# A pooled-attention and routed-experts kernel: record writes taken at a denser rhythm, and a first stage in another order

## The chip, the core and the metric

The kernel runs on one core of a Trainium2 chip. The metric is the device time of one execution in microseconds (us); the time before is the median of three runs. The profile is of one further execution. In it PE is TensorE (PEld its weight loads), DVE VectorE, ACT ScalarE, POOL GpSimd, SP SyncE; L637 is line 637 of the kernel.

## The reference

Eight batches of eight heads, 576 tokens, head dimension 64. Keys and values are averaged over blocks of eight tokens, so each query attends to 72 pooled keys:

```
k_p, v_p = means of k and v over 8 tokens          # 72 x 64 per head
attn     = softmax(q @ k_p.T / 8)
x        = attn @ v_p, heads side by side           # 4608 tokens x 512
noisy    = x @ w_gate + log(1 + exp(x @ w_noise)) * noise      # 8 experts
top2, w  = the two largest of noisy, softmax of the two
out[t]   = sum over the token's two experts of w * relu(x[t] @ w1[e]) @ w2[e]
```

Inputs and output are float32; w1 is 512 x 1024 and w2 1024 x 512 for each expert.

## The kernel before

The kernel has two large stages that overlap at their seam.

**Attention and routing.** The batches are taken in four pairs (pair 0 to 3), each pair in nine chunks (ci 0 to 8) of 128 tokens, 36 chunks in all. For a chunk, `qtr` turns q on TensorE and ScalarE copies it out (`qT`); `qk` makes scores for three groups of heads, VectorE takes the maximum (`mx`, L380) and ScalarE the exponentials; `et` turns these; `av` (L408) multiplies by values and, in the same matmul, by values already multiplied with the gate and noise weights, so that VectorE writes both the rows of x (`xr`, L419) and the router's partial logits (`lg`, L421). The rows go to DRAM (`x_dram`). The gate and noise weights reach that matmul through `wr` (loaded by `mid_consts`, L190) and `wrb`, six GpSimd copies of it (L196).

When a pair's last chunk is reached, `route` starts as a generator that is advanced two steps per chunk. GpSimd adds the heads' logits (L508, L509: "the adds"); VectorE begins at L516 and goes on through top-2; at L593 TensorE counts, for each token, its place in its expert's list (`rk`); VectorE then makes the records (L634 is its last instruction). For each pair there are 18 **record writes** (L637): indirect DMAs that GpSimd issues one by one, each of 128 records. They are put into a list, `scq`, from which `advance(n, m)` takes at most m at a time. Behind the writes of pairs 1, 2 and 3 stand, in the same list, the **record load** (L678) and the **row gathers** (L705) of expert 0's groups 0, 1 and 2: these groups take tokens only from the pairs already routed. A record write waits for a VectorE or ScalarE instruction of its chunk (`pace`).

**Experts.** For each expert there are three groups of up to four tiles of 128 rows. `split` (through `rows_of`) turns the gathered rows on TensorE (L755) and makes a high and a low part; `stage1` is x @ w1 in eight steps f (12 matmuls each, L1016); `stage2` is h @ w2, one tile t at a time (24 matmuls, L1127; L1093 for the last group of an expert). Expert 0's group 0 is turned in chunks 34 and 35 of the attention stage; groups 1 and 2 are turned from `hook`, inside stage 2 of the group before. The hooks `hook1` (per f) and `hook` (per t) also take records from `scq`, `hook1` as many as `POPS` says.

**Order.** The framework lays down each engine's instruction order when the program is built: by the order of the text, by readiness as it estimates it, and by explicit edges: `tc.issue_after(ins)` puts what is written under it behind `ins` on the same engine. On the chip every engine runs its list in order. So an instruction that waits holds up all behind it on its engine. GpSimd's list mixes adds, record writes, record loads and gathers; all loads of the first stage go through the SP queue in the order of the text.

With the pops as written, before the change, the list runs so: the 18 writes of pair 1 are taken from pair 2's ci 4 to pair 3's ci 4, ten of them before pair 2's adds are written into GpSimd's list; group 0's record load and gathers come at pair 3's ci 4; 11 writes of pair 2 come before the end of attention, the other 7, then group 1's load and gathers, in f 0 to 2 of group 0's stage 1; pair 3's 18 writes come in stage 2 of group 0 (5, 4, 4, 4) and at the head of group 1's stage 1 (1), there followed by group 2's load and gathers.

Of the kernel before, what the change touches and what calls it, by code (L numbers as in the profile page):

```python
# [8 lines left out]
F32 = mybir.dt.float32  # L9
# [4 lines left out]
OP = mybir.AluOpType  # L14
AX = mybir.AxisListType.X
# [4 lines left out]
def kernel(  # L20
# [12 lines left out]
    nc = tc.nc  # L33
# [149 lines left out]

    wrb = cp.tile([P, NSLOT, 2 * E], F32, name="wrb")

    def mid_consts():
        wr = cp.tile([P, H, 2 * E], F32, name="wr")
        for dup in range(2):
            for i, w in enumerate((moe_w_gate, moe_w_noise)):
                nc.sync.dma_start(wr[dup * 64:dup * 64 + 64, :, i * E:(i + 1) * E],  # L190
                                  w.rearrange("(h d) e -> d h e", d=D))
        nc.gpsimd.memset(wrb, 0.0)
        for n in range(NEB):
            rs = slice((n % 2) * 64, (n % 2) * 64 + 64)
            ns = len(HEADS[n])
            nc.gpsimd.tensor_copy(wrb[rs, SLOT0[n]:SLOT0[n] + ns, :],  # L196
                                  wr[rs, HEADS[n][0]:HEADS[n][0] + ns, :])

    KT, VT, QT, QR = {}, {}, {}, {}
    lastl, lasta = [None], [None]  # L200

    DK, DV = 0, 0
    PK, PV = 0, 0
# [75 lines left out]
    def v_prep(b):  # L279
        vt = VT[b]  # L280
        vs = ap_.tile([P, NEB, D], F32, tag="vs", name=f"vs{b}")
        VS[b] = vs
        if PV >> b & 1:
            halves(vt, b, BST, ((0, 3), (3, 6)), PV)
            yield
        yield from pooled(vs[:BST], vt, b, 0, NEB, BST, DV | PV)

    def pe_prep(b):
        ks = KS[b]
# [44 lines left out]
    def qtr(u, half, hp=None):  # L334
        kind, pr, b, jp = u
        if half == 0:
            QTT[u] = ap_.tile([P, H, P], F32, tag="qT", name=f"qT{pr}_{b}_{jp}", bufs=2)
        elif kind == "R":
            return
        qT = QTT[u]  # L340
        qp = ps2.tile([P, 4, P], F32, tag="one", name=f"qp{pr}_{b}_{jp}_{half}", bufs=2)
        for i in range(4):
            if kind == "R":
                src = QR[pr][:, 2 * i:2 * i + 2]
            else:
                src = QT[b][:, half * 4 + i, 2 * jp:2 * jp + 2]
            nc.tensor.transpose(qp[:, i], src.rearrange("p a d -> p (a d)"), ident)  # L347
        with tc.high_priority(offset=HP if hp is None else hp):
            nc.scalar.copy(qT[:, half * 4:half * 4 + 4], qp)

    def qk(u, g):
# [5 lines left out]
        if kind == "R":  # L357
            if g == 2:
                return
            if g == 0:  # L360
                SR[u] = [ps2.tile([P, 512], F32, tag="s", name=f"s{nm}_{k}", bufs=SB) for k in range(2)]
                for i in range(4):
                    for b2 in range(2):
                        for k in range(2):
                            nc.tensor.matmul(SR[u][k][b2 * 64:b2 * 64 + 64, i * G:(i + 1) * G],
                                             qT[k * 64:k * 64 + 64, i, b2 * 64:b2 * 64 + 64],
                                             kbd[b2][k * 64:k * 64 + 64, 2 * i + k, k * G:(k + 1) * G],
                                             start=True, stop=True)
            s = SR[u][g]
            rows = [(0, 2 * i + g) for i in range(4)]  # L370
        else:
            s = ps2.tile([P, 512], F32, tag="s", name=f"s{nm}", bufs=SB)
            rows = [(jj, h) for h in GRP[g] for jj in range(2)]
            for i, h in enumerate(GRP[g]):
                nc.tensor.matmul(s[:, i * 2 * G:(i + 1) * 2 * G], qT[:, h], kbd[b % 2][:, h],  # L375
                                 start=True, stop=True)
        n = len(rows)
        sv = s[:, :n * G].rearrange("p (r g) -> p r g", g=G)
        mx = ap_.tile([P, 6], F32, tag="mx", name=f"mx{nm}", bufs=4)
        nc.vector.tensor_reduce(out=mx[:, :n], in_=sv, axis=AX, op=OP.max, negate=True)  # L380
        for i, (jj, h) in enumerate(rows):
            lasta[0] = nc.scalar.activation(ex[:, jj, EPOS[h] * G:(EPOS[h] + 1) * G], sv[:, i], AF.Exp,  # L382
                                            bias=mx[:, i:i + 1])
# [103 lines left out]
    def drain(g):  # L487
        for _ in g:
            pass
# [322 lines left out]
    if WU:  # L812
        wu = ps2.tile([P, 512], F32, tag="s", name="wu", bufs=SB)
        for i in range(WU):
            nc.tensor.transpose(wu[:, i % 4 * P:(i % 4 + 1) * P], ident, ident)
    load_q(0)
    load_qr(0)
    load_v(0)
    block_tiles()
    mid_consts()  # L820
    drain(k_prep(0))
    load_k(1)
    load_q(1)
# [32 lines left out]
    for x in range(4):  # L856
        plan(34 + x // 2, lambda: next(splits))
    qtr(units[0], 0)
    qtr(units[0], 1)
    for g in range(3):  # L860
        qk(units[0], g)
    if ST & 1:
        qtr(units[1], 0, H0)
        qtr(units[1], 1, H0)
    drain(v_prep(0))
    if ST & 2:
        next(pg[0])
    else:
# [6 lines left out]
    for i, (ui, u, jj) in enumerate(chunks):  # L875
# [15 lines left out]

        def adv():
            pace[0] = lastx[0]
            advance(STEPS[pr], 2 if pr == NP - 1 and ci > 3 else quiet)

        for o in order + ("" if "b" in order else "b") + ("" if "x" in order else "x"):
            if o == "v" and i == 0:
# [58 lines left out]
    def split(grp):  # L956
        drain(rows_of(grp, bank))
# [192 lines left out]
                    wgens.pop(0)  # L1150

    s0 = SP_[0]
    POPS = {0: (4, 4, 2, 0, 0, 0, 0, 0), 1: (100, 0, 0, 0, 0, 0, 0, 0)}

    def hook1(i, f):
        if i == 0 and f == 0:
# [5 lines left out]
        advance(0, POPS[i][f])  # L1162

    def hook(i, t, mm):
        advance(0, (5, 4, 4, 4)[t] if i == 0 else 100)
        if t == 1 - i:
            with tc.issue_after(mm.ins):
                split(groups[i + 1])

    def flush(f):  # L1170
        if f == 3:
# [142 lines left out]
```

## Time and profile before

| | |
|---|---|
| median of three runs | 1024.56 us (1023.23 to 1025.97) |
| the profiled execution | 1026.55 us |
| its span, first to last instruction | 1024.7 us |
| granted clock of TensorE, mean | 0.990 |
| attention stage, first scores to the first matmul of L1016 | about 14 to 190.5 us |
| expert stage | 190.5 us to the end |

A row of a timeline gives the start in the span, the duration, the engine, the line, the operation, output<-inputs, and in brackets the idle time of the engine just before it with what ended it. Rows that follow one another on one engine and line are merged (x8 is eight instructions). A window row gives each engine's busy time in a stretch; the granted clock is a share of the full 2.4 GHz, so that 0.50 is the lower level of 1.2 GHz.

### The profile page before, as it was taken

The page shows a single profiled execution, that of the slowest core. Times are in us where ns is not written, and L with a number is a line of the kernel's source. Part 1 is how long each engine was busy: PE and PEld are TensorE (multiplying, and loading weights), DVE is VectorE, ACT ScalarE, POOL GpSimd, SP SyncE. Part 2 cuts the span into 40 slices and gives each one's busy share as a digit, 9 for nine tenths or more (in the row PEclk, how much of TensorE's full clock was granted, in tenths as well). Part 3 has the DMA queues.
Part 4 walks back from the last instruction along what each step waited for, and adds up shares of the span by engine and source line. Part 5 has one row for each costly group of instructions (what it writes and reads, how often), then busy time and mean ns, then how long its engine had stood idle before and what let it go on. Part 6 is the DMA issues. An engine that isn't in the chain of part 4 may idle for free.

```text
span 1024.7 us, 16468 instructions
## 1 busy us (share of the span) xinstructions
PE 990.3 (97%) x5832; PEld 886.4 (86%) x5832; DVE 548.3 (54%) x1261; ACT 344.1 (34%) x857; POOL 379.4 (37%) x433
## 2 busy tenths in 40 slices
PE   6999999898999999999999999999999999999996
PEld 5898898788898989898988898989888988898995
DVE  5799898572244455644464446444644455356341
ACT  4687787331113222411142124211421232123120
POOL 3023575646300442155115421551154215422514
PEclk9999999899899999999999999999999999999999
DMA  8989983361706755677267736772677357744624
GB/s 240 251 236 270 251 265 117 111 196 39 216 28 205 211 178 155 197 235 210 75 193 224 225 117 200 249 215 73 184 241 245 94 173 250 239 145 135 211 87 136
DMA packets 136006, 187.61 MB, mean 183 GB/s; under 512 B 29123, under 2 KB 84052, under 8 KB 135898
## 3 DMA queue, kind: packets, MB, share of 16 engines
q1 hardware_dynamic: 110458, 119.09, 39.9%
q0 software_dynamic: 25440, 67.05, 21.1%
q8 instruction: 72, 1.18, 0.5%
q14 instruction: 36, 0.29, 0.1%
HBM read 123.31 MB, written 70.74 MB: 189 GB/s over the span
## 4 chain that ended last, share of the span: by engine, by line
PE 82%; DMA 5%; DVE 4%; issue 3%; SPq 2%; POOL 2%; ACT 1%; POOLq 0%; DVEq 0%; ACTq 0%
PE bank L1016 34%; PE bank L1127 25%; PE bank L1093 10%; PE a L408 5%; PE s L375 3%; PE ep L393 2%; DMA wst<-in_moe_w_dram 2%; PE qp L347 1%; DMA xg<-x_dram,raw 1%; DMA qr<-in_q_dram 1%; DVE w L481 1%; SPq L219 1%; SPq L190 1%; POOL out_dram L1072 1%; DMA slot_dram<-ys 1%
## 5 line engine op out<-in xcount | busy, mean ns | idle before, releaser
L1016 PE MATMUL bank<-xh,w 128*128 128x512 f32 (+6 forms) x1536 | 390.4, 338 | 1.3 <-DVE pv L1064 1.3
L1016 PEld LDWEIGHTS bank<-xh,w 128*128 128x128 f32 x1536 | 270.3, 188 | 22.0 <-DVE pv L1064 1.7
L1127 PE MATMUL bank<-w,hh 128*128 128x512 f32 x880 | 272.7, 391 | 0.0
L1016 PE MATMUL bank<-xl,w 128*128 128x512 f32 (+6 forms) x768 | 259.7, 338 | 0.0
L1027 ACT ACTIVATE hh<-bank 128x512 fp32r<-128x512 f32 (+4 forms) x192 | 97.1, 508 | 458.4 <-PE bank L1016 435.0
L1028 DVE SCALAR_TENSOR_TENSOR hl<-bank,hh 128x512 fp32r<-128x512 f32 (+4 forms) x192 | 110.9, 579 | 242.8 <-ACT hh L1027 242.8
L1127 PEld LDWEIGHTS bank<-w,hh 128*128 128x128 f32 x880 | 165.9, 189 | 34.0
L1127 PE MATMUL bank<-w,hl 128*128 128x512 f32 x440 | 172.1, 391 | 0.1
L1016 PEld LDWEIGHTS bank<-xl,w 128*128 128x128 f32 x768 | 144.6, 188 | 10.3
L1064 DVE SCALAR_TENSOR_TENSOR pv<-bank,raw,pv 128x128 f32<-128x128 f32 x196 | 55.5, 342 | 109.6 <-PE bank L1127 61.9
L1068 POOL DMA_DIRECT2D slot_dram<-yt x17 | 9.8, 575 | 268.9 <-DVE yt L1064 217.4
L1093 PE MATMUL bank<-hh,w 128*128 128x240 f32 (+3 forms) x512 | 103.4, 298 | 2.1 <-DVE hl L1028 1.3
L1127 PEld LDWEIGHTS bank<-w,hl 128*128 128x128 f32 x440 | 83.0, 189 | 17.8 <-DVE hl L1028 0.5
L637 POOL DMA_INDIRECT rec_dram<-rec,pos x72 | 77.2, 1072 | 48.9 <-issue 14.2
L1048 POOL DMA_INDIRECT pv<-slot_dram,raw x70 | 68.5, 979 | 66.8 <-DMA slot_dram<-ys 34.9
L481 DVE TENSOR_TENSOR w<-wst,w 128x512 fp32r<-128x512 f32 x128 | 82.6, 682 | 10.4 <-ACT w L480 10.2
L1093 PEld LDWEIGHTS bank<-hh,w 128*128 128x128 f32 x512 | 82.5, 189 | 2.7 <-ACT hh L1027 1.6
L480 ACT CAST w<-wst 128x512 fp32r<-128x512 f32 x128 | 72.8, 618 | 27.5 <-DMA wst<-in_moe_w_dram 27.5
L714 POOL DMA_INDIRECT row<-x_dram,raw x70 | 70.0, 1000 | 21.9 <-issue 19.5
L1068 POOL DMA_DIRECT2D slot_dram<-pv x55 | 31.7, 577 | 123.7 <-DVE pv L1064 95.8
L1093 PE MATMUL bank<-hl,w 128*128 128x320 f32 (+3 forms) x256 | 75.9, 296 | 0.0
L382 ACT ACTIVATE ex<-s,mx 128x72 f32<-128x72 f32 x288 | 70.7, 344 | 9.7 <-DVE mx L380 9.6
(162 smaller groups left out, 1031.4 us busy)
## 6 DMA issues: line engine op xcount, KB each, us to landing
wst<-in_moe_w_dram SPq DMA_DIRECT2D x64, 512.0 KB
via<-row SPq DMA_DIRECT2D x266, 64.0 KB
xg<-via SPq DMA_DIRECT2D x63, 256.0 KB
slot_dram<-pv POOLq DMA_DIRECT2D x55, 256.0 KB, 3.7
x_dram<-xr SPq DMA_DIRECT2D x16, 512.0 KB
q<-in_q_dram SPq DMA_DIRECT2D x7, 1024.0 KB
k<-in_k_dram SPq DMA_DIRECT2D x6, 896.0 KB
v<-in_v_dram SPq DMA_DIRECT2D x12, 432.0 KB
```

What stands on the lines that cost most here:

```text
L382: lasta[0] = nc.scalar.activation(ex[:, jj, EPOS[h] * G:(EPOS[h] + 1) * G], sv[:, i], AF.Exp, bias=mx[:, i:i + 1])
L480: nc.scalar.copy(hv, sv)
L481: nc.vector.tensor_sub(lv, sv, hv.bitcast(F32))
L637: s = nc.gpsimd.indirect_dma_start(out=rec_dram[:, :], out_offset=bass.IndirectOffsetOnAxis(ap=pos[:, i, c:c + 1], axis=0), in_=rec[:, c, ...
L714: turn_of("pool", lambda: nc.gpsimd.indirect_dma_start(out=row[:32 * nr], out_offset=None, in_=x_dram[:, :], in_offset=bass.IndirectOffset ...
L1016: nc.tensor.matmul(part(ph), w1s(e, a, db, f), part(xs[b][:, db]), start=(i == 0), stop=(i == 3 * NDB - 1))
L1027: act = nc.scalar.activation(hh[:, :n], ph[:, :n], AF.Relu)
L1028: last = nc.vector.scalar_tensor_tensor(hl[:, :n], ph[:, :n], 0.0, hh[:, :n].bitcast(F32), op0=OP.max, op1=OP.subtract)
L1048: turn_of("pool", lambda: nc.gpsimd.indirect_dma_start(out=pv[:np_], out_offset=None, in_=slot_dram[:P + e * CAP, :], in_offset=bass.Indir ...
L1064: nc.vector.scalar_tensor_tensor(r_, y_, wc, pv[:plain] if plain else r_, op0=OP.mult, op1=OP.add)
L1093: nc.tensor.matmul(part(py), w2s(e, b, f)[:, mb * P:(mb + 1) * P], part(hs[f][a]), start=(i == 0), stop=(i == 3 * NFB - 1))
L1127: mm = nc.tensor.matmul(py, hs[f][a][:, cs], w2s(e, b, f), start=(i == 0), stop=(i == 3 * NFB - 1))
```

## The change

Three things are changed.

1. **First stage.** The gate and noise weights are no longer loaded in turned form (`wr`, four DMAs of 64 partitions x 8 heads x 8 values). They are loaded in rows of 512 values on eight partitions, twice side by side (four DMAs, right behind batch 0's v, into two of the buffers `wst`), and turned by 16 small TensorE transposes into one PSUM bank, from which one ScalarE copy makes `wr`; the six copies to `wrb` stay. The load of v of batch 0 is issued ahead of that of `qr`. The scores of the first three heads of the first unit are put in front of the transposes of q's second half; v of batch 0 is pooled in three parts (nine VectorE instructions in place of three), behind the maximum of the second head group.
2. **Rhythm of the record writes.** From pair 2 on, `adv` takes two records per chunk where it took one (in pair 3 already from ci 1). `POPS` for group 0's stage 1 becomes (8, 0, 0, 2, 3, 3, 3, 3).
3. **`hook`.** `split` of the next group is written ahead of `advance`, and after t = 0 of group 0 everything left in the list is taken.

With the pops as written, after the change: the 18 writes of pair 1 run from pair 2's ci 3 to pair 3's ci 1, 16 of them ahead of pair 2's adds; group 0's load and gathers come at pair 3's ci 1 and ci 2; 16 writes of pair 2 come before the end of attention, 2 more and group 1's load and gathers at f 0; pair 3's writes come at f 3 to f 7 (14) and t 0 (4), group 2's record load at t 0, its gathers at t 1 of group 0.

```diff
-    def mid_consts():
+    def mid_loads():
+        wt = [wp.tile([P, 2 * D * E], F32, tag="wst", name=f"wt{i}", bufs=WS) for i in range(2)]
+        for t, w in zip(wt, (moe_w_gate, moe_w_noise)):
+            for u in range(2):
+                nc.sync.dma_start(t[:H, u * D * E:(u + 1) * D * E], w.rearrange("(h d) e -> h (d e)", d=D))
+        nc.gpsimd.memset(wrb, 0.0)
+        return wt
+
+    def mid_consts(wt):
         wr = cp.tile([P, H, 2 * E], F32, name="wr")
-        for dup in range(2):
-            for i, w in enumerate((moe_w_gate, moe_w_noise)):
-                nc.sync.dma_start(wr[dup * 64:dup * 64 + 64, :, i * E:(i + 1) * E],
-                                  w.rearrange("(h d) e -> d h e", d=D))
-        nc.gpsimd.memset(wrb, 0.0)
+        wp_ = ps2.tile([P, 512], F32, tag="one", name="wps", bufs=2)
+        wv = wp_[:, :2 * E * H].rearrange("p (c h) -> p c h", h=H)
+        for i in range(2):
+            src = wt[i][:H].rearrange("h (d e) -> h e d", e=E)
+            for e in range(E):
+                nc.tensor.transpose(wv[:, i * E + e], src[:, e], ident[:H, :H])
+        nc.scalar.copy(wr, wv.rearrange("p c h -> p h c"))
...
-        yield from pooled(vs[:BST], vt, b, 0, NEB, BST, DV | PV)
+        for n0, n1 in ((0, 2), (2, 4), (4, 6)) if b == 0 else ((0, NEB),):
+            yield from pooled(vs[:BST, n0:n1], vt, b, n0, n1, BST, DV | PV)
...
     load_q(0)
+    load_v(0)
+    wt = mid_loads()
     load_qr(0)
-    load_v(0)
     block_tiles()
-    mid_consts()
...
     qtr(units[0], 0)
-    qtr(units[0], 1)
-    for g in range(3):
-        qk(units[0], g)
-    if ST & 1:
-        qtr(units[1], 0, H0)
-        qtr(units[1], 1, H0)
-    drain(v_prep(0))
+    qk(units[0], 0)
+    with tc.issue_after(lastqk[0].ins):
+        qtr(units[0], 1)
+    qk(units[0], 1)
+    mx1 = lastmx[0]
+    qk(units[0], 2)
+    qtr(units[1], 0, H0)
+    qtr(units[1], 1, H0)
+    with tc.issue_after(lastqk[0].ins):
+        mid_consts(wt)
+    with tc.issue_after(mx1.ins):
+        drain(v_prep(0))
...
-            advance(STEPS[pr], 2 if pr == NP - 1 and ci > 3 else quiet)
+            advance(STEPS[pr], 2 * quiet if pr >= NP // 2 else quiet)
...
-    POPS = {0: (4, 4, 2, 0, 0, 0, 0, 0), 1: (100, 0, 0, 0, 0, 0, 0, 0)}
+    POPS = {0: (8, 0, 0, 2, 3, 3, 3, 3), 1: (100, 0, 0, 0, 0, 0, 0, 0)}
...
     def hook(i, t, mm):
-        advance(0, (5, 4, 4, 4)[t] if i == 0 else 100)
         if t == 1 - i:
             with tc.issue_after(mm.ins):
                 split(groups[i + 1])
+        advance(0, (5, 100, 100, 100)[t] if i == 0 else 100)
```

## Rows read from the trace of the kernel before

**Rows 1.** The page's part on engines: busy time, share of the span, instructions.

```profile
PE 990.3 (97%) x5832; PEld 886.4 (86%) x5832; DVE 548.3 (54%) x1261; ACT 344.1 (34%) x857; POOL 379.4 (37%) x433
```

**Rows 2.** TensorE's timeline, 160 to 400: start, us, group, [idle before <- releaser].

```profile
177.09 0.43 PE L393 MATMUL ep<-ident,ex 128*112 128x128 f32 x2
...
181.91 1.95 PE L755 MATMUL xp<-ident,xg 128*128 128x128 f32 x8 [4.38 <-DMA xg<-x_dram,raw]
...
187.95 1.23 PE L755 MATMUL xp<-ident,xg 128*128 128x128 f32 x8
...
201.73 0.20 PE L593 MATMUL bank<-mb,before 128*128 128x80 bf16 x1
```

**Rows 3.** Timeline of all engines, 248 to 264.

```profile
252.97 0.39 PE L1127 MATMUL bank<-w,hl 128*128 128x512 f32 x1
...
261.46 1.13 PE L755 MATMUL bank<-ident,xg 128*128 128x128 f32 x4 [0.76 <-DMA xg<-x_dram,raw]
...
262.24 1.20 PE L1127 MATMUL bank<-w,hh 128*128 128x512 f32 x2
```

**Rows 4.** Windows: each engine's busy time, then granted clock, DMA share, GB/s.

```profile
184.00:185.00 1.00, 1.00 (x5) 1.00 (x4) 0.84 (x2) 1.00 (x3) 0.69 (x2) 0.50 0.43 151
...
264.00:265.00 1.00, 1.00 (x4) 0.71 (x3) 0.00 (x0) 0.00 (x0) 0.17 (x1) 0.50 0.78 221
```

**Rows 5.** GpSimd's timeline, 100 to 420.

```profile
131.13 0.97 POOL L637 DMA_INDIRECT rec_dram<-rec,pos  x1 [6.54 <-ACT eT L395]
132.41 2.45 POOL L637 DMA_INDIRECT rec_dram<-rec,pos  x1 [0.30 <-issue]
...
145.74 0.97 POOL L637 DMA_INDIRECT rec_dram<-rec,pos  x1 [0.30 <-issue]
...
146.73 3.50 POOL L508 TENSOR_TENSOR lg<-lg 128x512 f32<-128x512 f32 x2
...
168.60 0.97 POOL L637 DMA_INDIRECT rec_dram<-rec,pos  x1 [3.65 <-ACT ex L382]
...
171.05 0.59 POOL L678 DMA_DIRECT2D raw<-rec_dram  x1 [1.48 <-DMA rec_dram<-rec,pos]
...
174.52 1.00 POOL L705 DMA_INDIRECT xg<-x_dram,raw  x1 [0.30 <-issue]
...
190.48 1.30 POOL L508 TENSOR_TENSOR lg<-lg 128x512 f32<-128x512 f32 x1
...
213.37 0.58 POOL L678 DMA_DIRECT2D raw<-rec_dram  x1 [4.43 <-DMA rec_dram<-rec,pos]
...
217.99 1.00 POOL L705 DMA_INDIRECT xg<-x_dram,raw  x1 [4.04 <-DMA raw<-rec_dram]
...
247.90 0.96 POOL L637 DMA_INDIRECT rec_dram<-rec,pos  x1 [0.31 <-issue]
...
253.14 1.00 POOL L705 DMA_INDIRECT xg<-x_dram,raw  x1 [4.28 <-PE bank L1127]
...
256.99 0.95 POOL L705 DMA_INDIRECT xg<-x_dram,raw  x1 [0.31 <-issue]
```

**Rows 6.** VectorE's timeline, 118 to 250: three steps of routing.

```profile
153.02 0.23 DVE L516 SCALAR_TENSOR_TENSOR rt<-rt 128x72 f32<-128x72 f32 x1 [0.62 <-POOL rt L509]
...
170.87 0.15 DVE L634 TENSOR_TENSOR rec<-rt,tok 128x18 int32<-128x18 f32 x1
...
195.17 0.23 DVE L516 SCALAR_TENSOR_TENSOR rt<-rt 128x72 f32<-128x72 f32 x1 [3.12 <-POOL rt L509]
```

**Rows 7.** Windows of four microseconds in the first stage, columns as in rows 4.

```profile
16.00:20.00 4.00, 2.63 (x17) 2.25 (x16) 2.41 (x3) 3.19 (x13) 0.96 (x1) 1.00 0.71 74
...
20.00:24.00 4.00, 2.73 (x20) 2.23 (x19) 3.63 (x8) 2.63 (x10) 2.20 (x6) 1.00 1.03 386
```

**Rows 8.** Timeline of all engines, 0 to 45.

```profile
13.16 1.09 PE L347 MATMUL qp<-ident,q 128*128 128x128 f32 x4 [1.36 <-DMA q<-in_q_dram]
...
15.73 0.61 DVE L380 TENSOR_REDUCE mx<-s 128x6 f32<-128x432 f32 x1 [4.67 <-PE s L375]
...
19.04 3.22 POOL L196 COPY wrb<-wr 64x32 f32<-64x32 f32 x6 [12.17 <-DMA wr<-in_moe_w_noise_dram]
...
28.13 0.63 PE L347 MATMUL qp<-ident,qr 128*128 128x128 f32 x4 [0.34 <-DMA qr<-in_q_dram]
```

More of the change, by code (lines that the diff above doesn't have):

```diff
@@ L199 @@
     KT, VT, QT, QR = {}, {}, {}, {}
-    lastl, lasta = [None], [None]
+    lastl, lasta, lastqk, lastmx = [None], [None], [None], [None]
     DK, DV = 0, 0
@@ L346, in qtr @@
                 src = QT[b][:, half * 4 + i, 2 * jp:2 * jp + 2]
-            nc.tensor.transpose(qp[:, i], src.rearrange("p a d -> p (a d)"), ident)
+            lastqk[0] = nc.tensor.transpose(qp[:, i], src.rearrange("p a d -> p (a d)"), ident)
         with tc.high_priority(offset=HP if hp is None else hp):
@@ L374, in qk @@
             for i, h in enumerate(GRP[g]):
-                nc.tensor.matmul(s[:, i * 2 * G:(i + 1) * 2 * G], qT[:, h], kbd[b % 2][:, h],
-                                 start=True, stop=True)
+                lastqk[0] = nc.tensor.matmul(s[:, i * 2 * G:(i + 1) * 2 * G], qT[:, h], kbd[b % 2][:, h],
+                                             start=True, stop=True)
         n = len(rows)
@@ L379, in qk @@
         mx = ap_.tile([P, 6], F32, tag="mx", name=f"mx{nm}", bufs=4)
-        nc.vector.tensor_reduce(out=mx[:, :n], in_=sv, axis=AX, op=OP.max, negate=True)
+        lastmx[0] = nc.vector.tensor_reduce(out=mx[:, :n], in_=sv, axis=AX, op=OP.max, negate=True)
         for i, (jj, h) in enumerate(rows):
```

## The prediction

> **What bounds the kernel now.** I read the page first, then TensorE's timeline, then the lists of the engines that it waits for. The page says that TensorE is busy for 97% of the span [rows 1]; so what can be won lies in the rest, and in work done at the low clock. In the timeline of the seam and of expert 0, TensorE waits long in two places.
>
> *Stall 1, group 0's rows.* TensorE ends a group at 177.52 and then waits 4.38 us, to 181.91, for the gather of x rows [rows 2]. After it the granted clock is 0.50 [rows 4]; with that level up to about 187.5 the 5.6 us from 181.91 on do the work of half, so 2.8 us more are lost. Price: 7.2 us.
>
> *Stall 2, group 2's rows.* Stage 2 of group 1 ends its first tile at 253.36; the next begins at 262.24 [rows 3]. In these 8.9 us lie 16 transposes; eight take 1.23 us at the full clock [rows 2], so 16 take 2.5 and 6.4 us are waiting. Behind it the clock is again at 0.50 [rows 4], up to about 266, which loses half of 3.8 us, 1.9. Price: 8.3 us.
>
> Both wait for GpSimd's list. Group 0's record load is at 171.05, its first gather at 174.52; group 2's last record write ends at 248.86, the gathers go from 253.14 to 256.99, and the last lands at 261.45, 4.5 us after its issue [rows 3, 5]. The stages after that keep TensorE full, so what is won at 262 should arrive at the end.
>
> The third place is the start: VectorE idles 4.67 us before the first maximum at 15.73 [rows 8], and the DMA engines move 74 GB/s in 16 to 20 although they are 71% busy, against 386 GB/s in the next four microseconds [rows 7]; there the weights' 2048 pieces of 32 bytes are under way.
>
> **The change part by part.**
>
> *First stage.* Removed: the loads in small pieces. What stands behind them in SP's queue (k, q and the rest of q of batch 1) can land earlier, but the wait that shows is small, 0.34 us at 28.13 [rows 8]. Scores first: the transposes of q's second half wait for q until 13.16, and the first maximum follows 2.6 us later; with scores that need only q's first half, up to these 2.6 us come off VectorE's idle time. Added: 16 transposes (0.15 us each at most [rows 2], 2.5 together, where TensorE has 1.4 us idle of 4 [rows 7]), one ScalarE copy, and six more VectorE instructions; the smallest step of routing takes 0.23 us [rows 6], so 1.4 at most. The six copies to `wrb` remain, 3.22 us from 19.04 on [rows 8]; their cause is now TensorE's transposes behind the second unit's, and not a load, so they hardly begin earlier. Ends: 3.9 us lost, if nothing hides the new work, to 4.7 won, if the whole idle time goes. I take 2.0 won, nearest to the 2.6 of the scores.
>
> *Stall 1.* Group 0's load and gathers move up by two to three chunks. GpSimd then does, from 131.13 on, 16 writes of pair 1, pair 2's adds, two writes, the load, four gathers. Ten writes took 15.6 us here (131.13 to 146.73), 1.56 each; a write in a quiet stretch takes 0.96 + 0.31 = 1.27 [rows 5]. So: 25.0 + 6.3 (adds, 146.73 to L516 at 153.02 [rows 5, 6]) + 2.5 + load 0.9 and its two waits, 1.5 before it and 2.6 behind it (3.5 from issue to gather, less the 0.9) = 38.8: the first gather goes at 169.9 and not at 174.5, and with its 7.3 us of flight (174.52 to about 181.8 [rows 2, 5]) lands at 177.2, just ahead of TensorE's 177.5. Stall 1 goes: 7.2.
>
> *Stall 2.* Pair 3's writes move up from stage 2 into stage 1 of group 0, but GpSimd's list is one queue, and becomes dense. I sum it from 131.13 to group 2's gathers: 16 writes at 1.56 (25.0), 38 at 1.27 (48.3), adds of pair 2 6.3, of pair 3 3.4 (190.48 to 195.17, less a write inside), ten gathers at 1.28 (12.8), two loads and, priced like them, the stores of two tiles' rows that stand in between, at 0.9 each (3.6), and the waits around the loads: 4.1, 4.43 + 4.04, and 4.28 for group 2 [rows 5, 6], 16.9 in all. That is 116.3 us; the last gather goes at 246.2 and lands at 250.6, against 261.45: 10.9 earlier. TensorE without stall 1 would be there at 253.36 - 7.2 = 246.2; it still waits some 2.6 us in pieces, and ends the transposes at 251.3, 10.9 before 262.24. Whether the clock falls in that remnant decides over another 0 to 1.9; I take 0.
>
> *What is late next.* Six more writes stand ahead of pair 2's adds in GpSimd's list. VectorE's first routing step (L516, 153.02) waited 0.62 us for them [rows 6], so it is at its limit now. Behind it on VectorE stand maxima and rows of x, for which ScalarE and TensorE wait. Call the extra wait D. If the order that the build lays down foresees none of it, D is 6 x 1.56 = 9.4; if it foresees all, 0. I take what an order reckoned at the quiet price would miss, 6 x (1.56 - 1.27) = 1.7. D moves attention, and the rest of GpSimd's list with it, one for one.
>
> Sum: 10.9 + 2.0 - 1.7 = 11.2 us. The profiled execution took 1026.55 us, 1.85 more than its span and 2.0 more than the median; so 1015.4 on its terms, and **1013.4 us** on the median's. In general the time is 1011.7 + D.
>
> *A rule against the change.* While pair 1's records are written and VectorE is at its fullest, the spacing of the writes is 1.56 us on the mean, and one took 2.45; in the quiet stretch it is 1.27 [rows 5]. The Trainium skill, SBUF — State Buffer, section "Who interferes with whom", says that GpSimd and VectorE share a port pair under an exclusive lock, and that a DMA issued from GpSimd stalls for want of descriptors while VectorE holds it. By that rule the denser writes of pairs 1 and 2 should each wait for VectorE; the trace agrees in direction, with 0.29 us each, and at that the rule changes nothing in the sum above. It has its case below.
>
> **The rivals.**
>
> *Both stalls gone whole.* For it: if the 16 writes keep the quiet spacing, the list is 16 x 0.29 = 4.6 us shorter, and TensorE at 246.2 finds the rows there. Against it: TensorE's count (`rk`, 201.73 [rows 2]) comes right behind VectorE's chain that begins at 195.17 after waiting 3.12 us for GpSimd [rows 6]; without stall 1 TensorE is there 7 us earlier. Won: 7.2 + 8.3 + 2.0 = 17.5; 1007.1.
>
> *Given back on VectorE.* D near 9.4, because L516 keeps its place in VectorE's list: 1021.1. Or the same size at `rk`, where pair 3's adds stand behind 14 writes of pair 2 that can't begin before their records exist, at 171.0 [rows 6]: 171.0 + 14 x 1.27 = 188.8, about as late as before, so that the 7.2 of stall 1 come back at 201.7. For it: the order of writes ahead of adds is seen in the trace (145.74, then 146.73 [rows 5]).
>
> *Slower: the writes stretch.* Place: GpSimd's 16 writes ahead of pair 2's adds. If each took what the longest took, 2.45 + 0.30 [rows 5], they would need 44 us in place of 15.6, D would be 28 and the time 1040. It decides from D = 12.9, a spacing of 1.78 us (16 x 1.78 - 15.6), for slower than before, and from 1.97 us for slower by 0.3%. For it: ten writes already vary between 0.97 and 2.45. Against it: the mean. The Trainium skill's rule on the shared port (SBUF — State Buffer, "Who interferes with whom") would have this outcome if VectorE held the port through most of each write.
>
> *No change.* The gathers don't come earlier, since a record write waits for an instruction of its chunk anyway (3.65 us for an exponential at 168.60 [rows 5]), and the start gains nothing: 1024.6.
>
> **How the numbers follow.** A difference of 0.3% (3.1 us: 1021.5 and 1027.6) is about what a measurement of this kernel can tell from none. Chances: forecast, D from 0 to 5, 1010 to 1017: 0.45. Both stalls gone whole, 1004 to 1010: 0.20. Given back, 1017 to 1023: 0.20, a third of it above 1021.5. No change: 0.08. Slower: 0.07. So faster 0.45 + 0.20 + 0.13 = 0.78, same 0.07 + 0.08 = 0.15, slower 0.07. The range must leave out 0.2: above it, no change, slower and the end of given back, 0.15 to 0.18; below it, the best of both stalls gone with the start's full 4.7: 1007.1 - 2.7 = 1004.4. I give 1004.5 to 1022.0; the forecast's own range is 1010 to 1017.
>
> **What the profile after would show.** Right: TensorE's wait before the first transposes of group 0's rows under 1 us and no granted clock of 0.50 there; group 0's gather some 5 us earlier; the second wait down from 6.4 us to about 3, its gathers at 240 to 247; the first maximum at about 13.4. Wrong: L516 of pair 2 waiting over 5 us for GpSimd's adds, with TensorE idle behind it; `rk` of pair 3 with several us of idle in front; write spacings of 1.8 us and more in pairs 1 and 2; the first `av` later than now, which would put the fault in the weights' new way through TensorE, ScalarE and GpSimd.

## The result, and the profile after

The changed kernel takes 1030.18 us (median of 11 runs, 1026.85 to 1036.64) where the kernel before takes 1024.56 in the same set (11 runs): ratio 1.0064, 95% interval 1.0043 to 1.0084. It is slower by some 6 us; the forecast was 1013.4.

The profiled execution took 1030.17 us. The head of its page (first part of each line: busy us, share of the span, instructions), against [rows 1]:

```profile
span 1028.2 us, 16508 instructions
...
PE 992.4 (97%) x5848; PEld 891.4 (87%) x5848; DVE 546.4 (53%) x1267; ACT 343.5 (33%) x858; POOL 374.7 (36%) x433
```

TensorE is busy 2.1 us longer, part of it at the low clock, and the span is 3.5 us longer. Where the waits are now, in TensorE's timeline of the changed kernel, is to be read against [rows 2, 3]:

```profile
158.13 1.22 PE L376 MATMUL s<-kbd,qT 64*64 64x72 f32 x14 [5.90 <-ACT ex L393]
...
184.90 1.23 PE L766 MATMUL xp<-ident,xg 128*128 128x128 f32 x8 [0.26 <-ACT eT L406]
...
209.21 0.23 PE L604 MATMUL bank<-mb,before 128*128 128x80 bf16 x1 [6.88 <-DVE mb L577]
```

Both stalls of before are gone: the transposes of group 0's rows wait 0.26 us for an eviction and no longer for the gather, and between 211 and 287 no idle time over 0.5 us is left. In their place stand two new waits, 5.90 us at pair 2's scores and 6.88 us at the count of pair 3. Who is waited for is one step back, in VectorE's timeline (L527 is the routing step that was L516 in [rows 6]):

```profile
156.97 0.23 DVE L527 SCALAR_TENSOR_TENSOR rt<-rt 128x72 f32<-128x72 f32 x1 [6.46 <-POOL rt L520]
...
202.65 0.23 DVE L527 SCALAR_TENSOR_TENSOR rt<-rt 128x72 f32<-128x72 f32 x1 [9.96 <-POOL rt L520]
```

The same two steps waited 0.62 and 3.12 us before. L520 is the last of the routing adds on GpSimd; what stands ahead of them is GpSimd's timeline, against [rows 5]:

```profile
129.52 0.98 POOL L648 DMA_INDIRECT rec_dram<-rec,pos  x1 [7.25 <-DVE rec L645]
...
152.45 0.97 POOL L648 DMA_INDIRECT rec_dram<-rec,pos  x1 [0.30 <-issue]
153.45 2.06 POOL L519 TENSOR_TENSOR lg<-lg 128x512 f32<-128x512 f32 x2
155.59 0.45 POOL L520 TENSOR_TENSOR rt<-lg 128x128 f32<-128x128 f32 x1
...
162.05 0.59 POOL L689 DMA_DIRECT2D raw<-rec_dram  x1 [1.44 <-DMA rec_dram<-rec,pos]
164.96 1.02 POOL L716 DMA_INDIRECT xg<-x_dram,raw  x1 [2.32 <-DMA raw<-rec_dram]
...
178.42 1.01 POOL L648 DMA_INDIRECT rec_dram<-rec,pos  x1 [6.49 <-DVE rec L645]
...
197.96 1.30 POOL L519 TENSOR_TENSOR lg<-lg 128x512 f32<-128x512 f32 x1
...
252.83 0.95 POOL L716 DMA_INDIRECT xg<-x_dram,raw  x1 [0.30 <-issue]
```

Sixteen writes stand from 129.52 to 153.4, so pair 2's adds begin at 153.45 and not at 146.73; the late routing delays pair 2's records to 178.42 (before: 171.95), and pair 3's adds, behind fifteen writes of them, begin at 197.96 and not at 190.48. The gathers gain what was meant: group 0's first at 164.96 (before 174.52), group 2's last at 252.83 (before 256.99).

The waits cost more than their own length. Windows of the changed kernel (the number behind the five engines is the granted clock):

```profile
150.00:160.00 10.00, 4.10 (x42) 3.27 (x41) 2.62 (x9) 3.86 (x16) 7.34 (x11) 0.75 0.18 63
160.00:170.00 10.00, 10.00 (x64) 9.17 (x63) 6.41 (x30) 5.58 (x17) 5.09 (x6) 0.74 0.36 114
200.00:210.00 10.00, 3.12 (x22) 2.42 (x21) 5.95 (x27) 3.42 (x10) 5.75 (x11) 0.81 0.01 0
210.00:220.00 10.00, 10.00 (x39) 8.07 (x39) 10.00 (x38) 6.46 (x13) 2.81 (x3) 0.85 0.59 192
```

With the clock at 1.2 in place of 2.4 GHz for a time behind each wait, 160 to 170 lost 2.6 us (0.26 of ten) and 210 to 220 lost 1.5; the busy ends of the windows ahead of them (158.13 to 160 and 209.21 to 210, taken at half) lost 0.9 and 0.4, so 5.4 in all.

A third place is new: ahead of expert 1's last second stage TensorE stops for 3.48 us, and VectorE, which is named, had done its work (its last `hl` at 392.38).

```profile
391.06 0.27 PE L1032 MATMUL bank<-xh,w 128*128 128x240 f32 x1
394.81 0.75 PE L1109 MATMUL bank<-hh,w 128*128 128x240 f32 x2 [3.48 <-DVE xt L772]
```

The kernel before has a short stop near there, 0.74 us, 2.6 us into that second stage:

```profile
395.55 0.49 PE L1093 MATMUL bank<-hh,w 128*128 128x240 f32 x2 [0.74 <-issue]
```

The clock falls here too, in the changed kernel and not in the one before:

```profile
392.00:394.00 2.00, 0.00 (x0) 0.00 (x0) 2.00 (x3) 0.60 (x1) 0.00 (x0) 0.99 0.99 260
394.00:396.00 2.00, 1.19 (x5) 1.22 (x6) 1.89 (x4) 0.64 (x2) 0.00 (x0) 0.50 0.62 196
398.00:400.00 2.00, 2.00 (x11) 2.00 (x11) 1.01 (x2) 0.40 (x1) 0.00 (x0) 0.50 0.01 4
```

It is 0.50 from 394 to 400, which costs some 2.6 us more (half of the 5.2 from 394.81 on).

So far one can see that both stalls were won, and that two waits and a pause came for them. The seam comes out even: the first copy `hh` of expert 0's third group, ScalarE's first output of a group's first stage, comes at 271.6 us in the changed kernel and 271.8 in the one before. At expert 1's third group the changed kernel is 1.8 us ahead (382.0 and 383.8), and at expert 2's first 3.5 behind (411.5 and 408.0), as at the end. So in these two executions the two waits used up what the stalls gave, and the third place makes the whole of the loss. Which part of the change brings what is the experiments' to say.

### The profile page after: what moved, and what is told of

It reads as the page before. It is cut to its first block, busy times and chain, and to the rows that moved or that the text cites. A ratio compares the mean times of both kernels' runs of the same rounds, so it can differ in the third digit from the quotient of the medians.

```text
span 1028.2 us, 16508 instructions
## 1 busy us (share of the span) xinstructions
PE 992.4 (97%) x5848; PEld 891.4 (87%) x5848; DVE 546.4 (53%) x1267; ACT 343.5 (33%) x858; POOL 374.7 (36%) x433
## 3 DMA queue, kind: packets, MB, share of 16 engines
q8 instruction: 72, 1.18, 0.5%
## 4 chain that ended last, share of the span: by engine, by line
PE 87%; POOL 4%; issue 3%; DMA 3%; DVE 2%; ACT 1%; SPq 0%; POOLq 0%; ACTq 0%; DVEq 0%
PE bank L1032 37%; PE bank L1143 28%; PE bank L1109 10%; PE a L419 4%; PE s L386 2%; PE ep L404 2%; POOL rec_dram L648 2%; PE qp L358 1%; DMA wt<-in_moe_w_gate_dram 1%; DMA rec_dram<-rec,pos 1%; POOL lg L519 1%; POOL out_dram L1088 1%; PE s L376 1%; DMA k<-in_k_dram 0%; PE kT L309 0%
## 5 line engine op out<-in xcount | busy, mean ns | idle before, releaser
L1109 PE MATMUL bank<-hh,w 128*128 128x240 f32 (+3 forms) x512 | 105.9, 303 | 4.8 <-DVE xt L772 3.5
L1109 PEld LDWEIGHTS bank<-hh,w 128*128 128x128 f32 x512 | 84.9, 194 | 5.3 <-ACT xh L777 3.6
```

The lines of the kernel that those rows point to most:

```text
L1109: nc.tensor.matmul(part(py), w2s(e, b, f)[:, mb * P:(mb + 1) * P], part(hs[f][a]), start=(i == 0), stop=(i == 3 * NFB - 1))
```

## The experiments

Four sets of kernels, each with the kernel before in it. In the first two sets every kernel that the others repeat took 1.1 to 1.6% longer than there. Their traces show pauses of single engines, at different moments between some 95 and 270 us, that nothing in the trace explains (in `before_again` TensorE 1.30 us at 102.0, VectorE 1.51 at 140.6 and ScalarE 2.23 at 265.9; in `rhythm_only` TensorE 3.36 at 200.4). So each is compared with before of its own set, and points in time with those of its set alone. Two landmarks serve throughout: the first copy `hh` of ScalarE in expert 0's groups 0, 1 and 2 (they show how the seam is left), and the stretch E1 from the first `hh` of expert 1's third, last group to that of expert 2's first, in which the third place lies (the expectation of `before_dummy16` names it by the second and the third group; its numbers are those of this stretch).

**Set 1: the parts alone.** The theory: dense writes ahead of the adds make the loss. The rival: the first stage does.

`start_only`: the changed kernel's first stage, with

```diff
-            advance(STEPS[pr], 2 * quiet if pr >= NP // 2 else quiet)
+            advance(STEPS[pr], 2 if pr == NP - 1 and ci > 3 else quiet)
-    POPS = {0: (8, 0, 0, 2, 3, 3, 3, 3), ...
+    POPS = {0: (4, 4, 2, 0, 0, 0, 0, 0), ...
```

and `hook` as before. 

> The kernel before with the new first stage alone (weights turned on TensorE, scores first, v of batch 0 in parts); the order of the record writes is that of before. Theory (the loss comes from the record writes that stand ahead of the routing adds in GpSimd's list): no idle time of 5 us at the scores near 158 and none at the count rk near 205; 1 us or so won at 119, so 1022 to 1025, within 0.3% of before. Rival (the first stage costs, through TensorE, ScalarE or the late weights): 1028 or more, with the loss visible before 119.

`rhythm_only`: before, with these three places as in the change. 

> The kernel before with the new rhythm of the record writes alone (two for each step in pairs 2 and 3, other numbers in expert 0, group 2's gathers ahead of a step's writes); the first stage is that of before. Theory: TensorE waits about 6 us at pair 2's scores near 158 (the adds of pair 2 stand behind 16 writes) and about 7 us at rk near 209; the waits of before at 182 and 257 to 262 are gone; about the time of the changed kernel plus the 1 us of the start, 1028 to 1033. Rival (the first stage costs): 1021 to 1026.

`adv_alone`: the changed kernel with `POPS` and `hook` of before. 

> The changed kernel with the numbers and the order in expert 0 (POPS and hook) put back; the two writes for each step in pairs 2 and 3 stay. Theory: the waits near 158 (about 6 us) and at rk (about 7 us) stay, because the writes ahead of the adds are the same; the wait for group 2's rows (before: 6.4 us) comes back in part or whole, as pair 3's writes go out later; 1030 to 1037, slower than the changed kernel or equal. Rival (the loss comes from the numbers in expert 0, whose writes crowd the stages there): the wait at rk shrinks and the time falls to 1022 to 1026.

`hooks_alone`: the changed kernel with the `advance` line of before. 

> The changed kernel with the number of writes for each step in pairs 2 and 3 put back to that of before; first stage and the numbers in expert 0 stay. Theory: no wait of 6 us near 158, the wait for group 0's rows near 182 is back at about 4 us, rk without a wait above 2 us, and group 2's rows earlier by some us; 1016 to 1023, faster than before. Rival (the numbers in expert 0 cost): a wait of 5 us or more in expert 0 that neither kernel before has, 1027 or more.

Measured, ratio to before (1039.82 us) with its interval, then the landmarks in us:

| kernel | ratio | groups 0, 1, 2 | E1 |
|---|---|---|---|
| start_only | 1.0053 (1.0033 to 1.0074) | 208.7, 256.6, 285.6 | 25.6 |
| rhythm_only | 1.0094 (1.0068 to 1.0119) | 222.1, 272.0, 297.0 | 24.3 |
| adv_alone | 1.0139 (1.0106 to 1.0172) | 218.4, 264.7, 294.0 | 27.3 |
| hooks_alone | 1.0036 (1.0012 to 1.0060) | 206.4, 258.6, 285.3 | 25.7 |

Both held in part. The two kernels with two writes for each step enter expert 0 some 10 to 16 us later than the two without. But the way is not the one that I expected: in both, VectorE's first routing step of pair 2 waits 0.42 us for the adds, and the count of pair 3 doesn't wait at all. TensorE stands 7.50 us ahead of the second rows of group 0, and has pauses of 1 to 3 us without a releaser. So this set shows that the denser writes come with a late seam, and not by which wait. `hooks_alone` was to be faster than before by the theory (1016 to 1023), and is 0.4% slower; but `start_only`, which has the same first stage, is slower by no less without the numbers of expert 0, so these cost nothing that can be seen. The first stage alone is slower by some 5 us, which I had put at 1 us won: the rival is right too.

**Set 2: the same chip for before, after and the first stage; and a first cure.**

`before_again`, `after_again` and `start_again` repeat three kernels. 

> The kernel before, unchanged, for a profile taken on the same chip as the other kernels of this set. All theories: the two waits of before (for group 0's rows, 4 to 5 us, and for group 2's rows, about 6 us in all) stand in it.

 

> The changed kernel, unchanged, beside the kernel before on the same chip. Theory (the record writes ahead of the routing adds): ratio to before 1.004 to 1.009 again, with the waits near 158 (about 6 us) and at rk (about 7 us); the 3.5 us ahead of expert 1's last group at 395 are chance and need not come again. Rival (that wait in expert 1 belongs to the change): it comes again at the same place with 3 us or more.

 

> The kernel before with the new first stage alone, once more, now with a profile of before from the same chip. If the first stage itself costs: TensorE behind before by 3 us or more already at the first unit's end (before 60 us), ratio 1.005 again. If it gains its 1 us and the loss comes later, by the moved order of instructions: level with before or ahead of it at 60 us, and 4 us or more behind at 200. If the loss was of that chip alone: a ratio within 0.3% of 1.

`pair1_single_rk_late`: two edits of the changed kernel,

```diff
-            advance(STEPS[pr], 2 * quiet if pr >= NP // 2 else quiet)
+            advance(STEPS[pr], 2 * quiet if pr == NP - 1 else quiet)
 ...
         elif i == 0:
             next(rt, None)
-            next(rt, None)
```

> The changed kernel with two edits: pair 1's records are again written one for each step (ten ahead of pair 2's adds in place of sixteen), and the count rk of pair 3 stands two eighths of group 0's first stage later on TensorE. Theory: no wait of 5 us near 158, rk's wait under 3 us, group 0's rows with a wait under 2 us, group 2's rows without one; some 12 us less than the changed kernel, 0.6 to 1.0% faster than before. Rival (the denser writes as such cost, or the first stage does): a time within 3 us of the changed kernel.

| kernel | ratio to before (1036.28 us) | groups 0, 1, 2 | E1 |
|---|---|---|---|
| before_again | (one run, 1038.44 us) | 207.2, 251.5, 282.6 | 25.1 |
| after_again | 1.0043 (1.0018 to 1.0068) | 216.1, 258.5, 282.7 | 27.2 |
| start_again | 1.0037 (1.0015 to 1.0058) | 208.3, 255.2, 283.8 | 27.3 |
| pair1_single_rk_late | 1.0051 (1.0028 to 1.0074) | 215.0, 263.2, 288.0 | 27.7 |

`before_again` is a single run, read for its trace alone. The changed kernel enters expert 0 8.9 us late and has it all back at group 2 (in the first profiles 204.0 against 196.5, then 271.6 against 271.8); here too the loss comes in expert 1: 0.4 us ahead at its third group, 1.7 behind at expert 2's first. The two waits of 6 and 7 us that I expected to find again aren't there: VectorE's first routing steps wait 0.42 us in pair 2 and 2.95 in pair 3, and TensorE stands 4.98 us ahead of the second rows of group 0. The instructions and their order are those of the first profile, so the same program loses its time in these sets at other places, and what sets off the pauses may hide the waits. The 3.48 us in expert 1 did not come back in that size, but E1 is again longer than before's. My cure, from which I expected 0.6 to 1.0% less than before, failed: group 0 is 1.1 us earlier than in `after_again`, and groups 1 and 2 are 5 us later. That fits the list, in which eight writes now stand behind the adds and ahead of group 0's record load:

```profile
176.89 0.59 POOL L689 DMA_DIRECT2D raw<-rec_dram  x1 [2.49 <-DMA rec_dram<-rec,pos]
177.47 0.13 POOL L576 MEMSET mb<- 128x8 bf16 x1
180.00 1.01 POOL L716 DMA_INDIRECT xg<-x_dram,raw  x1 [2.40 <-DVE rec L597]
...
186.95 1.00 POOL L648 DMA_INDIRECT rec_dram<-rec,pos  x1 [2.16 <-ACT eT L406]
```

Its first gather goes at 180.00 where `after_again` has it at 175.4. In this run the adds and the gathers traded places. Part of this loss may be the set's pauses (VectorE stops 1.41 and 0.84 us, without a releaser, in pair 2's routing); since the wait at pair 2's scores that the cure was to take away is not in `after_again` either, the run, within 1 us of it as the rival had it, decides nothing.

**Set 3: the adds out of the list, and the first stage's instructions.**

`after_adds_vec`: the changed kernel, `before_adds_vec`: the kernel before, both with

```diff
-                nc.gpsimd.tensor_add(lg[:, a:b, :h], lg[:, a:b, :h], lg[:, a:b, h:2 * h])
+                V.tensor_add(lg[:, a:b, :h], lg[:, a:b, :h], lg[:, a:b, h:2 * h])
-            nc.gpsimd.tensor_add(L[:, a - c0:b - c0], lg[:, a:b, 0], lg[:, a:b, 1])
+            V.tensor_add(L[:, a - c0:b - c0], lg[:, a:b, 0], lg[:, a:b, 1])
```

> The changed kernel with the routing adds on VectorE in place of GpSimd, so that no record write stands ahead of them; else unchanged. Theory (the two new waits come from adds that stand behind the denser writes): the wait of 6 us at pair 2's scores goes, pair 3's count comes some 7 us earlier, and expert 0's first group starts 6 to 9 us earlier than in the changed kernel, at some 2 us for each pair on VectorE; 5 to 8 us less than the changed kernel, ratio to before 0.997 to 1.000. Rival (VectorE is full there and only takes the wait over): ratio 1.003 or more, expert 0's start within 2 us of the changed kernel's.

 

> The kernel before with the routing adds on VectorE. Theory: before waits for the adds by 0.6 us in pair 2 and 3.1 us in pair 3 on VectorE, and stands behind TensorE's other waits for rows; within 0.3% of before, 1.5 us either way. Rival (moving the adds is a gain or a loss by itself): more than 0.4% either way, and then the run above must be read against this one.

`before_dummy16`: the kernel before, with

```diff
+    dm = ps2.tile([P, 512], F32, tag="one", name="dm", bufs=2)
+    for i in range(16):
+        nc.tensor.transpose(dm[:, i * 8:(i + 1) * 8], ident[:8, :], ident[:8, :8])
     drain(v_prep(0))
```

> The kernel before with 16 more transposes of 8 columns on TensorE in the first stage, whose result is not used, at the place where the new first stage turns its weights; nothing else. From the first ScalarE copy of expert 1's second group to that of its third group the kernels with the old first stage took 24.2 to 25.1 us, those with the new one 25.6 to 29.5. If the added TensorE instructions do it (they shift the point of the program at which TensorE needs its next block of instructions): 26 us or more there, ratio 1.002 to 1.004. If something else of the first stage does it: 25 or less there, ratio within 0.2% of 1.

`start_wu0`: `start_only` with `WU = 0` for `WU = 16`. 

> The new first stage alone (record writes as before) without the 16 warm-up transposes at the very start, so that TensorE's count of instructions from there on is that of before. If the count does it: 24 to 25 us at the place in expert 1, and some 2 us less than the first stage with its warm-up, less what the colder start costs (1 to 2 us, seen before 30 us). If it is not the count: 25.6 us or more there.

| kernel | median us | ratio to before (1023.57 us) | groups 0, 1, 2 | E1 |
|---|---|---|---|---|
| after_adds_vec | 1011.25 | 0.9876 (0.9859 to 0.9893) | 186.8, 229.5, 254.5 | 27.1 |
| before_adds_vec | 1022.64 | 0.9986 (0.9971 to 1.0000) | 195.2, 238.0, 270.9 | 23.6 |
| before_dummy16 | 1026.26 | 1.0024 (1.0013 to 1.0036) | 197.4, 238.8, 269.7 | 27.3 |
| start_wu0 | 1031.47 | 1.0062 (1.0039 to 1.0086) | 204.1, 246.2, 278.6 | 25.7 |

This settles what the adds behind the writes cost. Moved to VectorE, the adds are worth at most 3 us to the kernel before, and 0.0188 of 1024.56, 19.3 us, to the changed one, where I had expected 5 to 8. VectorE's timeline of `after_adds_vec` shows the adds of pair 2 and the routing step behind them, of pairs 2 and 3, without a wait:

```profile
144.69 0.68 DVE L519 TENSOR_TENSOR lg<-lg 128x512 f32<-128x512 f32 x1
...
146.20 0.41 DVE L519 TENSOR_TENSOR lg<-lg 128x256 f32<-128x256 f32 x1
...
151.52 0.22 DVE L527 SCALAR_TENSOR_TENSOR rt<-rt 128x72 f32<-128x72 f32 x1
...
185.47 0.24 DVE L527 SCALAR_TENSOR_TENSOR rt<-rt 128x72 f32<-128x72 f32 x1
```

And TensorE's windows of it have neither a stall nor a low clock from 140 to 260:

```profile
140.00:160.00 20.00, 19.82 (x180) 18.28 (x179) 18.45 (x59) 17.56 (x60) 14.82 (x13) 1.00 0.56 179
160.00:180.00 20.00, 19.14 (x159) 17.05 (x159) 17.29 (x69) 16.50 (x54) 13.09 (x14) 1.00 0.61 173
180.00:200.00 20.00, 19.64 (x104) 16.25 (x103) 18.20 (x65) 8.41 (x19) 11.79 (x16) 1.00 0.42 122
200.00:220.00 20.00, 20.00 (x94) 16.72 (x93) 14.98 (x54) 8.15 (x15) 15.73 (x15) 1.00 0.66 197
220.00:240.00 20.00, 20.00 (x135) 18.55 (x134) 5.11 (x15) 3.03 (x8) 12.99 (x16) 1.00 0.42 106
240.00:260.00 20.00, 20.00 (x109) 18.16 (x108) 6.73 (x16) 3.50 (x8) 6.58 (x8) 1.00 0.80 227
```

The first stage: sixteen transposes whose result nobody uses cost 2.5 us (0.0024). At expert 0 the kernel with them is 0.9 us behind before's first profile and at group 2 ahead of it (269.7 and 271.8), and E1 is 27.3 against 24.2 us. So in its one profile the time goes not where they stand but in expert 1; as its span (1024.6) is no longer than that of before (1024.7), the profile doesn't show the cost whole. TensorE's timeline of `before_dummy16` in expert 1:

```profile
389.47 0.27 PE L1019 MATMUL bank<-xh,w 128*128 128x240 f32 x1
392.23 0.56 PE L1096 MATMUL bank<-hh,w 128*128 128x240 f32 x2 [2.49 <-DVE xt L761]
```

It is the third place of the changed kernel, at the same step of the program. `start_wu0`, whose count of instructions is that of before, has a pause of 2.49 us as well, 5.5 us further on (404.30 to 406.79, within that second stage), and E1 is 25.7. By the mark that I had set (24 to 25 if the count does it, 25.6 or more if not) it speaks against the count alone.

**Set 4: what the pause hangs on, and the cure without the first stage.**

`rhythm_adds_vec`: `rhythm_only` with the adds on VectorE. 

> The kernel before with the new rhythm of the record writes and with the routing adds on VectorE; the first stage is that of before. Measured so far: the changed kernel with the adds on VectorE 0.9876 of before, the new first stage alone 1.004 to 1.005. If the new first stage costs by itself (2.5 us through its 16 more TensorE instructions, seen in expert 1, and no gain at the start): some 3 us less than the changed kernel with the adds on VectorE, 0.983 to 0.986, with 25 us or less at the place in expert 1. If it costs only together with the old order of writes: 0.987 to 0.990.

`before_dummy64`, `before_dummy128`: 64 and 128 unused transposes in place of 16. 

> The kernel before with 64 unused transposes of 8 columns on TensorE in the first stage. They cost time there; only the place in expert 1 is looked at. If the pause there follows from where the point of the program falls at which TensorE's next block of instructions is fetched, it changes with the number: with 64 more it may come before or behind, and is not the 2.5 us of 16 more, or the fetch stands elsewhere against it. If each more instruction only makes it worse: 2.5 us or more.

 

> The same with 128 unused transposes. A block fetched for TensorE is 16 KB by the profile (72 packets of 1.18 MB); if an instruction has 64 bytes and a transpose two of them (a weight load and a matmul), 128 transposes are one block, and the pause in expert 1 is again that of before, 0 to 0.8 us, with the fetch 1 to 2 us ahead of it. If the place of the block does not matter: 2.5 us or more, as with 16.

`rhythm_adds_vec`: 1008.50 us, ratio 0.9835 (0.9812 to 0.9858), groups 188.6, 231.3, 256.3, E1 23.5. It beats both kernels, by 16.9 us against before.

The two kernels with more transposes are single runs, of which only the traces are read. With 64 the pause is split into two of 1.04 us (E1 25.4), in TensorE's timeline:

```profile
393.22 0.46 PE L1096 MATMUL bank<-hh,w 128*128 128x240 f32 x2 [1.04 <-DVE hl L1031]
397.74 0.27 PE L1096 MATMUL bank<-hl,w 128*128 128x240 f32 x1 [1.04 <-issue]
```

With 128 there is none (E1 23.1); windows of that stretch:

```profile
396.00:398.00 2.00, 2.00 (x20) 2.00 (x19) 0.53 (x2) 0.88 (x2) 1.42 (x2) 1.00 0.85 264
398.00:400.00 2.00, 2.00 (x20) 2.00 (x20) 1.15 (x3) 0.44 (x1) 1.45 (x2) 1.00 0.85 242
400.00:402.00 2.00, 2.00 (x20) 2.00 (x20) 2.00 (x3) 0.78 (x2) 0.00 (x0) 1.00 0.70 213
```

So the pause doesn't grow with the number of instructions; it seems to go by where in the program that number puts the next block of them. The trace has the blocks as packets of a DMA queue (the page: 72 packets, 1.18 MB, 16 KB each). In quarters of a microsecond, the packet of the changed kernel lies in 391.50 to 391.75:

```profile
q8 instruction: 1, 0.02, 38.5%
```

TensorE stops at 391.33 there and goes on at 394.81, 3.2 us after the packet. In the kernel before the packet lies in 393.00 to 393.25, TensorE works on to 394.8 and goes on at 395.55, 2.5 us after it; with 16 more it is 389.50 and 392.23, with 64 more 390.25 and 393.22, then 395.00 and 397.74. The packet is followed 2.5 to 3.2 us later by the end of the pause each time; what differs is how far TensorE could work on. With 128 more the packet lies at 396.75 and there is no pause behind it.

Whose block it is can be counted. Between the packets at 406.00, 434.75 and 460.75 of the kernel before TensorE runs 129 and 133 matmuls with nearly as many weight loads:

```profile
406.00:434.75 28.75, 28.75 (x129) 23.79 (x128) 17.71 (x26) 11.92 (x22) 4.92 (x6) 1.00 0.63 199
434.75:460.75 26.00, 26.00 (x133) 23.62 (x132) 10.63 (x27) 5.57 (x11) 13.28 (x13) 1.00 0.78 229
```

With 128 transposes more, the packets come 127 or 128 matmuls later at six of the eight places from 375 to 465, and 73 packets come in place of 72. So these packets follow TensorE's program, with some 128 matmuls and their weight loads in each. From 375.75 to 406.00 the next ones come after only 69, 61, 25, 31 and 52 matmuls. This is around an expert's last group, each step of which the program holds in three versions, of which one runs, by the count of the expert's rows. TensorE passes over the others, and so comes sooner to the end of a block. That this is why the pause stands here is argued, not shown; the last groups of the other experts have no pause over 0.55 us.

## Why the prediction was wrong, step by step

- **Stall 1 and stall 2 go: right.** Neither wait is in the profile after. Their price held as well where the adds are out of the way: 7.2 and 8.3 us make 15.5, and `rhythm_adds_vec`, which has the new rhythm, the adds on VectorE and the old first stage, wins 16.9 us (14.5 to 19.3 by its interval), 1.4 of which moving the adds gives to the kernel before. In the profiles it is 6.6 us ahead of `before_adds_vec` at group 0 and 14.6 at group 2, so 6.6 and 8.0 for the two stalls. The sum of GpSimd's list had put both at 10.9. In `after_adds_vec` group 2's last gather goes at 235.7, ten microseconds ahead of the 246.2 that I summed; but 9.7 of these are the adds, which my sum holds and that list doesn't. Whether 10.9 would have held with the adds in the list and on time, no run shows.
- **What is late next: this step failed.** I bounded the extra wait D at pair 2's first routing step by 0 and 9.4 us, took 1.7 "as an order reckoned at the quiet price would miss", and treated the wait at pair 3's count as another way in which the same size could come back. Measured, the step waits 6.46 us (0.62 before), the one of pair 3 9.96 (3.12 before), and both reach TensorE: 5.90 and 6.88 us, 12.8 together, and 5.4 us of low clock behind them. So the first step came 5.8 us later than before, within my bounds, and the second 6.8, which my D didn't hold. These two waits are the signs of being wrong that I had named, and both came. D, measured as the changed kernel less its copy with the adds on VectorE, is 19.3 us where I had 1.7. My formula was 1011.7 + D, and with D taken away 0.9876 of 1024.56 is 1011.9; that these agree is luck, since the stalls gave 4.6 us more than I summed, the moved adds 1.4, and the first stage 6.2 less.
- Why it was too low: nothing in the trace spoke for an order that foresees the writes. The timeline [rows 5] showed ten writes ahead of the adds and VectorE's [rows 6] 0.62 us of waiting behind them; six more at the 1.56 us that I had read there are 9.4, and that was the plain reading (153.45 against 146.73 is 6.7 later). Then I didn't carry it on: late routing makes late records, these make late writes, and behind them stand the next pair's adds. One in-order list with a loop through two other engines delays twice.
- **Given back on VectorE, the rival with 0.20, was the right mechanism,** priced at 1021.1 for one of its two places. As both places came, and the first stage lost, the time went to 1030.
- **First stage, 2.0 us won: right where it stands, wrong in the sum.** The first maximum comes at 13.2 to 13.7 us in nine profiles with the new stage; with the old one at 15.73 [rows 8], but at 13.7 to 14.1 in the four other profiles of kernels that have it unaltered: I had read an outlier as the rule. At the fourteenth maximum 0.8 us are left (mean 52.4 of eight profiles, `start_wu0` left out, against 53.2 of five; each has a spread of 2 us). And `after_adds_vec` enters expert 0 1.8 us ahead of `rhythm_adds_vec`, yet ends 2.8 behind (1011.25 and 1008.50). I had costed its 16 transposes by their duration in the first stage. They cost 2.5 us (shown by `before_dummy16`). That they do so through the pause in expert 1 is argued: E1 is 27.2 us on the mean of nine profiles with 16 more TensorE instructions and 24.1 on that of five without, but `start_wu0`, with the count of before, has 25.7. Where the rest of the 3.8 to 5.5 us goes isn't settled.
- **The writes stretch: no.** The sixteen took 23.9 us, 1.50 each, less than the 1.56 of before. The rule from the Trainium skill that stood behind that rival (SBUF — State Buffer, section "Who interferes with whom": VectorE and GpSimd share a port pair under an exclusive lock) shows itself here in GpSimd's adds, not in its writes: the first two took 3.50 us while VectorE worked [rows 5], and 2.06 us in the changed kernel, where VectorE stood still waiting for them; VectorE's own addition of v beside them took 3.46 us before (146.18) and 1.75 in the changed kernel (145.07). The spacing of the writes doesn't go by VectorE's load alone: in `after_adds_vec` fifteen follow one another from 169.49 to 189.23 at 1.32 us on the mean, with VectorE busy for 84%.
- **Sum.** Stalls 15.5 won, first stage 4.2 lost (0.9876 less 0.9835, from two sets, so give or take some 3 us), D in the size that is left, 17.9 lost: 6.6 us slower, as measured. The 17.9 is the remainder; 12.8 us of waits and 5.4 us of low clock make 18.2, which agrees with it. The result lies outside the range because D and the first stage both erred to the slow side, by more than the stalls erred to the fast one, and because the only rival beyond the range on the slow side was a third thing.

## What to carry to other kernels

When an edit makes an in-order queue denser, look for what else that queue carries: here six small adds for each pair stood behind the writes, two other engines waited for them, and moving them to another engine turned 0.6% lost into 1.2% won. Follow the delay once around the loop (late adds, late records, late writes, late adds of the next round) before a bound is halved. And look for the price of added instructions also where they don't stand: sixteen of them in the first stage go with a pause of TensorE some 370 us further on, where the kernel passes over code that it doesn't run.

## What the hardware showed that I had not expected

- TensorE pauses for 0.74 to 3.48 us around expert 1's last group. The pause begins between 0.2 us ahead of an instruction packet and 1.9 us behind its start, and roughly it is the longer the earlier it begins. 16, 64 and 128 further instructions of TensorE in the first stage gave 2.49, twice 1.04, and no pause. The packets follow the count of TensorE's matmuls, some 128 to a packet where the code runs straight and 25 to 69 where versions not run are passed over. That the late block makes the pause is argued from this. The load on the DMA engines doesn't make it alone: their share was 0.97 to 1.01 in most of the pauses, but 0.01 in the second of `before_dummy64` and 0.09 around that of `start_wu0`, and with 128 more it was 0.85 behind the packet without a pause.
- The same adds take VectorE 0.68 and 0.41 us for 512 and 256 columns and GpSimd 1.30 and 0.76.
- The same kernel before took 1023.6 us in one set and 1039.8 in another on the same chip, with pauses of 1 to 3 us of one engine or another, between some 95 and 270 us, that have no releaser in the trace. What they are stays open.
